# A decode-step attention and gated-FFN kernel: the tile framework's ordering replaced by the order of the source

## The chip, the cores and the metric

The kernel runs on one core of a Trainium2 chip, in one launch. The metric is device time in microseconds, lower is better. Five engines work beside one another, each through its own queue of instructions: PE (TensorE, matrix products), DVE (VectorE), ACT (ScalarE), POOL (GpSimd) and SP (SyncE, which here only issues DMA transfers). They order themselves by semaphores. Sixteen DMA engines carry the transfers between HBM and the on-chip memory SBUF; products land in PSUM.

## The reference

One token `x` of 576 numbers is normalized, and two blocks are added to it: attention of 32 heads against a cache of 8192 keys and values per head, and an FFN with 4608 units whose gate is a ReLU.

```python
def _A_ref(x, k_cache, v_cache, wq, wo):          # H, Sk, Dh = 32, 8192, 128; D = 576
    q = (x @ wq).reshape(B, Sq, H, Dh).transpose(0, 2, 1, 3)
    scores = jnp.einsum("bhqd,bhkd->bhqk", q, k_cache) * (Dh ** -0.5)
    p = _softmax(scores, axis=-1)
    o = jnp.einsum("bhqk,bhkd->bhqd", p, v_cache)
    return o.transpose(0, 2, 1, 3).reshape(B, Sq, H * Dh) @ wo

def _B_ref(x, W_gate, W_up, W_down):              # F = 4608
    gate = jnp.einsum("bsd,df->bsf", x, W_gate)
    up = jnp.einsum("bsd,df->bsf", x, W_up)
    gate = gate * (gate > 0)
    return jnp.einsum("bsf,fd->bsd", gate * up, W_down)

xn = _layernorm(x)
return x + _A_ref(xn, ...) + _B_ref(xn, ...)
```

All is float32. Each cache holds 32 x 8192 x 128 numbers, 134 MB; a unit whose gate isn't positive adds nothing, so its up and down weights needn't be read.

## The kernel before, in words

**The stream.** Nearly all bytes come through one ring of five SBUF slots (`NST = 5`, `stream`, L46 to L50). SP issues one DMA for each tile, and a slot is asked for anew when the tile in it has been used up. In the order of issue: three tiles of wq and three of the gate weights (`wg`), then for each of four groups of eight heads (`NG = 4`, `G = 8`) eight K tiles and eight V tiles of 4096 KB each, a *head tile* each, and at the end seven ever smaller tiles of wo (8, 8, 8, 4, 2, 1 and 1 heads).

**Setup and gate.** DVE normalizes x (L85 to L91) and spreads it over the partitions as `xb`. Then `dot` (L97 to L99) multiplies 128 rows of weights with it and sums: 32 dots give q (into the zero-filled `qz`), 36 give the gate for 36 chunks of 128 units (`FC = 36`). L113 to L119 make the ReLU of it (`gr`) and `idx`, the numbers of the rows to fetch; a unit with a closed gate gets a number out of range.

**FFN.** For each chunk, `fetch` (L135 to L141) has POOL gather the 128 rows of up and down weights, 4608 bytes a row, into one of three buffers `gb` (`NB = 3`); numbers out of range move nothing. `ffn(c)` (L143) then does the *up product* on DVE (`dot` with the gate as scale, result `hh`) and the *down product* on PE (`rows`, 4 products into `acc`, L129, which the profile counts as 8). `fetch` for chunk c + 3 follows it in the source.

**Attention.** `scores` (L169) multiplies a K tile by q on PE, 16 products a tile (32 in the profile, L178), for all eight heads of a group into one PSUM tile `s`. `softmax` (L183) is a chain over DVE, PE and ACT. `values` (L210) multiplies a V tile by the probabilities (L220), has DVE copy the result (`oc`, L223) and PE turn it into columns (`ot`, L225).

**What sets the order.** After every head tile the source calls `between` (L160), which puts in an `ffn` when

```python
passed += 1
if used < FC and (passed - FIRST) * FC >= (used + 1) * SPAN:
    ffn(used)
```

with `FIRST = 4` and `SPAN = 58`. The text of the source is not the order in which the engines get their instructions, though: the kernel is written in a tile framework, which records what depends on what, then arranges the instructions by a planner of its own, engine by engine, gives out the buffers and sets the semaphores. Each engine then takes its queue strictly in order.

Of the kernel before, what the change touches and what calls it, by code (L numbers as in the profile page):

```python
# [2 lines left out]

# [12 lines left out]
P = 128  # L16
D = 576
# [9 lines left out]
NST = 5  # L27
NB = 3
FIRST = 4
SPAN = 58  # L30
RQ = 11
RG = 12
# [3 lines left out]
@with_exitstack  # L36
def tile_block(ctx: ExitStack, tc: tile.TileContext, x, kt, vt, wq, wg, ud, wo, out):
    nc = tc.nc
    cp = ctx.enter_context(tc.tile_pool(name="cp", bufs=1))
    st = ctx.enter_context(tc.tile_pool(name="st", bufs=NST))  # L40
    wk = ctx.enter_context(tc.tile_pool(name="wk", bufs=2))
    pk = ctx.enter_context(tc.tile_pool(name="pk", bufs=2, space=bass.MemoryType.PSUM))
    pv = ctx.enter_context(tc.tile_pool(name="pv", bufs=1, space=bass.MemoryType.PSUM))
    ps = ctx.enter_context(tc.tile_pool(name="ps", bufs=2, space=bass.MemoryType.PSUM))

    def stream(src):  # L46
        n = src.shape[-1]
        t = st.tile([P, n], F32, tag="st", name="st")
        nc.sync.dma_start(t, src)
        return t  # L50

    xa = cp.tile([1, D], F32, name="xa")
    nc.scalar.dma_start(xa, x)
    x4 = cp.tile([P, Q], F32, name="x4")
    nc.gpsimd.memset(x4, 0.0)
    nc.scalar.dma_start(x4[0:P:32, :], x.rearrange("o (j q) -> (o j) q", j=4))
    ident = cp.tile([P, P], F32, name="ident")
    make_identity(nc, ident)

    num = cp.tile([P, FC], F32, name="num")  # L60
    nc.gpsimd.iota(num, pattern=[[P, FC]], base=0, channel_multiplier=1, allow_small_or_imprecise_dtypes=True)
    eps = cp.tile([1, 1], F32, name="eps")
    nc.vector.memset(eps, EPS)
    one = cp.tile([1, P], F32, name="one")
    nc.vector.memset(one, 1.0)
    hs = cp.tile([P, G], F32, name="hs")
    nc.vector.reduce_sum(hs, ident.rearrange("p (j i t) -> p i j t", j=4, i=G), axis=AX.XY)
    sb = cp.tile([P, 4], F32, name="sb")
    nc.vector.reduce_sum(sb, ident.rearrange("p (j m) -> p m j", j=4)[:, :4, :], axis=AX.X)
    qz = cp.tile([P, H, 63], F32, name="qz")  # L70
    nc.gpsimd.memset(qz, 0.0)
    gb = [cp.tile([P, 2 * D], F32, name=f"gb{i}") for i in range(NB)]
    for t in gb:
        nc.gpsimd.memset(t, 0.0)  # L74
    po = [pv.tile([P, 512], F32, name=f"po{i}") for i in range(2)]
    acc = pv.tile([P, 512], F32, name="acc")
    for t in po + [acc]:
        nc.vector.memset(t, 0.0)


    sm = cp.tile([1, 8], F32, name="sm")
    xb = cp.tile([P, D], F32, name="xb")
    jk = cp.tile([P, D], F32, name="jk")
    xn = jk[:1, :]
    nc.vector.reduce_sum(sm[:, 0:1], xa, axis=AX.X)  # L85
    nc.vector.tensor_scalar_mul(sm[:, 1:2], sm[:, 0:1], 1.0 / D)
    nc.vector.tensor_scalar(xa, xa, sm[:, 1:2], None, op0=ALU.subtract)  # L87
    nc.scalar.activation(xn, xa, AF.Square, accum_out=sm[:, 2:3])
    nc.scalar.activation(sm[:, 3:4], sm[:, 2:3], AF.Sqrt, bias=eps, scale=1.0 / D)
    nc.vector.reciprocal(sm[:, 4:5], sm[:, 3:4])  # L90
    nc.vector.tensor_scalar_mul(xn, xa, sm[:, 4:5])  # L91
    for b in range(2):
        px = ps.tile([P, 512], F32, tag="sm", name="px")
        nc.tensor.matmul(px[:, :D // 2], one, xn[:, b * (D // 2):(b + 1) * (D // 2)], start=True, stop=True)  # L94
        nc.vector.tensor_copy(xb[:, b * (D // 2):(b + 1) * (D // 2)], px[:, :D // 2])

    def dot(rows, dst, scale=1.0):  # L97
        nc.vector.tensor_tensor_reduce(out=jk, in0=rows, in1=xb, scale=scale, scalar=0.0,  # L98
                                       op0=ALU.mult, op1=ALU.add, accum_out=dst)  # L99

    for s in range(0, H, RQ):
        n = min(RQ, H - s)
        t = stream(wq[:, s * D:(s + n) * D])
        for i in range(n):
            dot(t[:, i * D:(i + 1) * D], qz[:, s + i, 31:32])
    gate = cp.tile([P, FC], F32, name="gate")
    for s in range(0, FC, RG):
        t = stream(wg[:, s * D:(s + RG) * D])
        for i in range(RG):
            dot(t[:, i * D:(i + 1) * D], gate[:, s + i:s + i + 1])  # L110


    gr = cp.tile([P, FC], F32, name="gr")  # L113
    nc.vector.tensor_scalar(gr, gate, 0.0, None, op0=ALU.is_gt)
    nc.vector.tensor_mul(gr, gr, gate)
    off = cp.tile([P, FC], F32, name="off")
    nc.vector.tensor_scalar(off, gate, 0.0, float(2 * F), op0=ALU.is_le, op1=ALU.mult)
    idx = cp.tile([P, FC], I32, name="idx")
    nc.vector.tensor_add(idx, off, num)  # L119
    hh = cp.tile([P, FC], F32, name="hh")  # L120
# [4 lines left out]
    def rows(t, i, col):  # L125
        nonlocal done
        for j in range(4):
            c = i + j * Q
            nc.tensor.matmul(acc[32 * j:32 * j + 1, :Q], col, t[:, c:c + Q],  # L129
                             start=(done == 0), stop=(done == total - 1))  # L130
        done += 1

    fetched = 0

    def fetch():  # L135
        nonlocal fetched
        c = fetched
        t = gb[c % NB]
        nc.gpsimd.indirect_dma_start(t, None, ud, bass.IndirectOffsetOnAxis(ap=idx[:, c:c + 1], axis=0),  # L139
                                     bounds_check=F - 1, oob_is_err=False)  # L140
        fetched += 1  # L141

    def ffn(c):  # L143
        t = gb[c % NB]
        dot(t[:, :D], hh[:, c:c + 1], gr[:, c:c + 1])
        rows(t, D, hh[:, c:c + 1])

    def turned(rows, n):
        m = n // P
        pt = ps.tile([P, 4, P], F32, tag="sm", name="pt")  # L150
        for b in range(m):
            nc.tensor.transpose(pt[:, b, :], rows[:, b * P:(b + 1) * P], ident)  # L152
        return pt

    os = cp.tile([P, H], F32, name="os")
    used = 0

    passed = 0

    def between():  # L160
        nonlocal used, passed
        passed += 1
        if used < FC and (passed - FIRST) * FC >= (used + 1) * SPAN:
            ffn(used)
            used += 1
            if fetched < FC:
                fetch()

    def scores(g):  # L169
        s = pk.tile([P, 512], F32, tag="pk", name="s")  # L170
        for i in range(G):
            h = G * g + i
            t = stream(kt[h])
            for u in range(4):
                r = 4 * i + u
                for j in range(4):
                    c = (4 * u + j) * 512
                    nc.tensor.matmul(s[32 * j:32 * j + 32, :], qz[:, h, 31 - r:63 - r], t[:, c:c + 512],  # L178
                                     start=(r == 0), stop=(r == 31))
            between()  # L180
        return s

    def softmax(g, s):  # L183
        mr = wk.tile([P, 1], F32, name="mr")
        nc.vector.reduce_max(mr, s, axis=AX.X)  # L185
        pm = ps.tile([P, 512], F32, tag="sm", name="pm")
        nc.tensor.transpose(pm[:1, :P], mr, ident)
        hm = wk.tile([1, G], F32, name="hm")
        nc.vector.tensor_reduce(hm, pm[:1, :P].rearrange("p (j i t) -> p i j t", j=4, i=G), axis=AX.XY, op=ALU.max)
        hr = wk.tile([1, 4, G, 4], F32, name="hr")  # L190
        nc.vector.tensor_scalar_mul(hr, hm[:, None, :, None].to_broadcast([1, 4, G, 4]), -SCALE)
        pb = ps.tile([P, 512], F32, tag="sm", name="pb")
        nc.tensor.matmul(pb[:, :1], hr.rearrange("p j i t -> p (j i t)"), one[:, :1], start=True, stop=True)
        nb = wk.tile([P, 1], F32, name="nb")
        nc.vector.tensor_copy(nb, pb[:, :1])  # L195
        p = wk.tile([P, 512], F32, name="p")
        lr = wk.tile([P, 1], F32, name="lr")
        nc.scalar.activation(p, s, AF.Exp, bias=nb, scale=SCALE, accum_out=lr)  # L198
        pt = turned(p, 512)
        pT = wk.tile([P, P, 4], F32, name="pT")  # L200
        nc.vector.tensor_copy(pT, pt.rearrange("k b r -> k r b"))  # L201
        lb = wk.tile([P, P], F32, name="lb")
        nc.vector.tensor_copy(lb, lr.to_broadcast([P, P]))
        pl = ps.tile([P, 512], F32, tag="sm", name="pl")
        nc.tensor.matmul(pl[:, :G], lb, hs, start=True, stop=True)
# [24 lines left out]
    for _ in range(NB):  # L230
        fetch()
# [43 lines left out]
```

## Time and profile before

| what | value |
|---|---|
| time, median of 3 runs | 777.56 us (775.14 to 777.75) |
| time of the profiled execution | 777.12 us |
| its span, first to last instruction | 775.3 us |
| mean TensorE clock granted | 0.762 of full |
| busy: PE, DVE, POOL | 407.1, 122.3, 43.0 us |
| moved by DMA | 308.83 MB, 398 GB/s on the mean |

All stretches in the profile are in microseconds from the start of the span. Busy times say little by themselves here, as transfers and engines work at once; what counts is who waits for whom at which time, and whether the DMA engines have something to do. In a line such as "PE a L178 <- DMA b", the engine on the left stood idle until the one on the right was done. A group of instructions is named by its line, its engine, what it writes, an arrow and what it reads.

### The profile page before, as it was taken

The page shows a single profiled execution, that of the slowest core. Times are in us where ns is not written, and L with a number is a line of the kernel's source. Part 1 is how long each engine was busy: PE and PEld are TensorE (multiplying, and loading weights), DVE is VectorE, ACT ScalarE, POOL GpSimd, SP SyncE. Part 2 cuts the span into 40 slices and gives each one's busy share as a digit, 9 for nine tenths or more (in the row PEclk, how much of TensorE's full clock was granted, in tenths as well). Part 3 has the DMA queues.
Part 4 walks back from the last instruction along what each step waited for, and adds up shares of the span by engine and source line. Part 5 has one row for each costly group of instructions (what it writes and reads, how often), then busy time and mean ns, then how long its engine had stood idle before and what let it go on. Part 6 is the DMA issues. An engine that isn't in the chain of part 4 may idle for free.

```text
span 775.3 us, 6515 instructions
## 1 busy us (share of the span) xinstructions
PE 407.1 (53%) x2888; PEld 118.1 (15%) x2888; DVE 122.3 (16%) x291; ACT 8.0 (1%) x14; POOL 43.0 (6%) x48
## 2 busy tenths in 40 slices
PE   1003012234357855656666765566667656667664
PEld 0000000001112311111112211112121111121123
DVE  7994011112221100000100000001000000010000
ACT  2000000000000000000000000000000000000000
POOL 2001012233310000000000000000000000000000
PEclk9997556666679986686787677777786786786789
DMA  9999977786779999999999999999999999999995
GB/s 383 433 434 430 431 315 278 291 301 253 269 274 434 430 430 428 429 431 430 430 429 432 429 430 433 430 431 432 432 433 432 433 430 433 430 429 428 430 428 216
DMA packets 16317, 308.83 MB, mean 398 GB/s; under 512 B 4150, under 2 KB 4158, under 8 KB 6818
## 3 DMA queue, kind: packets, MB, share of 16 engines
q1 hardware_dynamic: 11096, 297.93, 90.0%
q0 software_dynamic: 5184, 10.49, 4.1%
q8 instruction: 22, 0.36, 0.2%
q14 instruction: 5, 0.04, 0.0%
q10 hardware_dynamic: 10, 0.00, 0.0%
HBM read 319.16 MB, written 0.00 MB: 412 GB/s over the span
## 4 chain that ended last, share of the span: by engine, by line
DMA 72%; PE 14%; DVE 10%; issue 2%; ACT 1%; POOL 0%; POOLq 0%; DVEq 0%; ACTq 0%
DMA st<-in_kt 33%; DMA gb<-in_ud,idx 16%; DMA st<-in_vt 16%; DVE jk L98 8%; PE po L220 7%; DMA st<-in_wo 6%; PE s L178 6%; PE ot L225 1%; PE acc L129 1%; DVE oc L223 0%; DVE xa L87 0%; PE pt L152 0%; ACT p L198 0%; PE px L94 0%; POOL gb L139 0%
## 5 line engine op out<-in xcount | busy, mean ns | idle before, releaser
L178 PE MATMUL s<-st,qz 128*32 128x512 f32 x1024 | 176.8, 854 | 138.7 <-DMA st<-in_kt 138.7
L220 PE MATMUL po<-st,pT 128*4 128x512 f32 x1024 | 161.2, 786 | 57.6 <-DMA st<-in_vt 55.0
L178 PEld LDWEIGHTS s<-st,qz 128*32 128x32 f32 x1024 | 41.3, 150 | 267.3 <-DMA st<-in_kt 111.4
L129 PE MATMUL acc<-gb,hh 128*1 128x144 f32 x288 | 19.1, 353 | 115.9 <-DVE hh L98 115.9
L223 DVE COPY oc<-po 128x512 f32<-128x512 f32 x32 | 22.1, 692 | 249.0 <-PE po L220 249.0
L220 PEld LDWEIGHTS po<-st,pT 128*4 128x4 f32 x1024 | 28.4, 102 | 162.2 <-issue 102.3
L98 DVE CUSTOM_DVE_ANT_0 jk<-st,xb 128x576 f32<-128x576 f32 x68 | 51.5, 757 | 2.4
L98 DVE CUSTOM_DVE_ANT_0 jk<-gb,xb,gr 128x576 f32<-128x576 f32 x36 | 29.5, 819 | 131.1 <-DMA gb<-in_ud,idx 130.4
L225 PE MATMUL ot<-sb,oc 128*128 128x1 f32 x256 | 33.7, 253 | 26.2 <-DVE oc L223 26.2
L139 POOL DMA_INDIRECT gb<-in_ud,idx x36 | 37.3, 1037 | 179.9 <-DVE idx L119 62.3
L225 PEld LDWEIGHTS ot<-sb,oc 128*128 128x128 f32 x256 | 31.0, 191 | 56.6 <-DVE oc L223 56.6
L185 DVE TENSOR_REDUCE mr<-s 128x1 f32<-128x512 f32 x4 | 2.8, 692 | 231.5 <-PE s L178 231.5
L129 PEld LDWEIGHTS acc<-gb,hh 128*1 128x1 f32 x288 | 4.4, 81 | 132.7 <-DVE hh L98 130.3
L129 PE MATMUL acc<-st,os 128*1 128x144 f32 x256 | 10.0, 313 | 7.0 <-DMA st<-in_wo 7.0
L198 ACT ACTIVATE p<-s,nb 128x512 f32<-128x512 f32 x4 | 2.7, 687 | 665.3 <-DVE nb L195 665.3
L129 PEld LDWEIGHTS acc<-st,os 128*1 128x1 f32 x256 | 6.5, 91 | 10.2 <-DMA st<-in_wo 8.3
L94 PE MATMUL px<-jk,one 1*128 1x288 f32 x4 | 2.3, 722 | 9.8 <-DVE jk L91 9.8
L152 PE MATMUL pt<-ident,p 128*128 128x128 f32 x16 | 3.5, 360 | 4.4 <-ACT p L198 4.4
L201 DVE COPY pT<-pt 128x512 f32<-128x512 f32 x4 | 2.8, 692 | 2.9 <-PE pt L152 2.9
L87 DVE TENSOR_SCALAR xa<-xa,sm 1x576 f32<-1x576 f32 x1 | 3.1, 3056 | 0.0
L74 POOL MEMSET gb<- 128x1152 f32 x3 | 3.0, 1047 | 0.0
L98 DVE DVE_READ_ACCUMULATOR2_ANT hh<- 128x1 f32 x36 | 3.0, 83 | 0.0
(48 smaller groups left out, 35.5 us busy)
## 6 DMA issues: line engine op xcount, KB each, us to landing
st<-in_kt SPq DMA_DIRECT2D x32, 4096.0 KB, 42.4
st<-in_vt SPq DMA_DIRECT2D x32, 4096.0 KB, 42.5
st<-in_wg SPq DMA_DIRECT2D x3, 3456.0 KB, 35.4
st<-in_wo SPq DMA_DIRECT2D x3, 2304.0 KB, 35.2
st<-in_wq SPq DMA_DIRECT2D x2, 3168.0 KB, 13.9
st<-in_wq SPq DMA_DIRECT2D x1, 2880.0 KB, 23.8
st<-in_wo SPq DMA_DIRECT2D x1, 1152.0 KB, 25.3
gb<-in_ud,idx POOLq DMA_INDIRECT x36, 11.7
```

The costliest lines, as they stand in the source:

```text
L74: nc.gpsimd.memset(t, 0.0)
L87: nc.vector.tensor_scalar(xa, xa, sm[:, 1:2], None, op0=ALU.subtract)
L98: nc.vector.tensor_tensor_reduce(out=jk, in0=rows, in1=xb, scale=scale, scalar=0.0, op0=ALU.mult, op1=ALU.add, accum_out=dst)
L129: nc.tensor.matmul(acc[32 * j:32 * j + 1, :Q], col, t[:, c:c + Q], start=(done == 0), stop=(done == total - 1))
L139: nc.gpsimd.indirect_dma_start(t, None, ud, bass.IndirectOffsetOnAxis(ap=idx[:, c:c + 1], axis=0), bounds_check=F - 1, oob_is_err=False)
L152: nc.tensor.transpose(pt[:, b, :], rows[:, b * P:(b + 1) * P], ident)
L178: nc.tensor.matmul(s[32 * j:32 * j + 32, :], qz[:, h, 31 - r:63 - r], t[:, c:c + 512], start=(r == 0), stop=(r == 31))
L185: nc.vector.reduce_max(mr, s, axis=AX.X)
L201: nc.vector.tensor_copy(pT, pt.rearrange("k b r -> k r b"))
L220: nc.tensor.matmul(o[32 * j:32 * j + 4, :], pT[:, row, :], t[:, c:c + 512], start=(u == 0), stop=(u == 3))
L223: nc.vector.tensor_copy(oc, o)
L225: nc.tensor.matmul(ot[:, i:i + 1], oc[:, b * P:(b + 1) * P], sb[:, b:b + 1], start=(b == 0), stop=(b == 3))
```

## The change

The same products, sums and transfers are issued without the framework. A class `Plan` takes each instruction with the names of what it reads and writes, and keeps every engine's instructions in the order in which the source gives them. Its `finish` works out which instruction must wait for which: not for one that the engine already knows to be done through an earlier wait, and on one engine not for reads before a write, nor at all on PE; a write after a write or a read after a write on DVE, ACT or POOL is waited for. All buffers are laid out by hand; those of the softmax are now single.

`between` has a new rule (`FIRST = 6`, `EVERY = 1.55`): the up product of chunk u goes out after head tile 6 + 1.55 u or the next one, its down product one head tile later, and the gather for chunk u + 3 right behind the down product. In `values`, the turning of a tile's result (`gather(i - 1)`, a name for the L225 products and no DMA) stands behind the products of the next tile. The normalized x is kept in `xa`; `hs`, `sb` and the clearing of three PSUM tiles come after the gate. The order of the stream and its five slots are as before. At the end SP waits for the output's transfer. The core of the diff:

```diff
+    def finish(self):
+        ops = self.ops
+        known = {e: {} for e in self.eng}
+        after = []
+        place = {e: 0 for e in self.eng}
+        for n, op in enumerate(ops):
+            e = op["engine"]
+            k = known[e]
+            waits = {}
+            for o, kind in sorted(op["needs"], reverse=True):
+                of = ops[o]
+                if of["sem"] is not None:
+                    key, at = ("dma", o), 1
+                else:
+                    if of["engine"] == e and (kind == "war" or e == "PE"):
+                        continue
+                    key, at = of["engine"], of["place"]
+                if k.get(key, 0) >= at:
+                    continue
+                waits[key] = max(waits.get(key, (0, 0)), (at, o))
+                for key2, at2 in after[o].items():
+                    k[key2] = max(k.get(key2, 0), at2)
+                k[key] = max(k.get(key, 0), at)
+            op["waits"] = [o for _, o in waits.values()]
+            place[e] += 1
+            op["place"] = place[e]
+            after.append(dict(k))
...
+        for n, op in enumerate(ops):
+            engine = self.eng[op["engine"]]
+            waits = [ops[o]["value"] for o in op["waits"]]
+            for s, v in waits[1:]:
+                engine.wait_ge(s, v)
+            i = op["emit"](engine)
+            if waits:
+                i.wait_op(*waits[0], "sem-ge")
+            if "value" in op:
+                i.then_inc(op["value"][0], 16 if op["sem"] is not None else 1)
...
 NST = 5
 NB = 3
-FIRST = 4
-SPAN = 58
 RQ = 11
 RG = 12
+FIRST = 6
+EVERY = 1.55
...
     def stream(src):
+        nonlocal tiles
+        s = tiles % NST
+        tiles += 1
         n = src.shape[-1]
-        t = st.tile([P, n], F32, tag="st", name="st")
-        nc.sync.dma_start(t, src)
-        return t
+        add("SP", lambda e: e.dma_start(slot[s][:, :n], src), writes=[("st", s)], sem=slot_sem[s])
+        return slot[s], ("st", s)
...
-    def dot(rows, dst, scale=1.0):
-        nc.vector.tensor_tensor_reduce(out=jk, in0=rows, in1=xb, scale=scale, scalar=0.0,
-                                       op0=ALU.mult, op1=ALU.add, accum_out=dst)
+    def dot(rows, key, dst, dkey, scale=1.0, extra=()):
+        add("DVE", lambda e: e.tensor_tensor_reduce(out=jk, in0=rows, in1=xb, scale=scale, scalar=0.0, op0=ALU.mult,
+                                                    op1=ALU.add, accum_out=dst),
+            reads=[key, ("xb", 0), ("xb", 1), *extra], writes=[dkey, "jk"])
...
-    def fetch():
-        nonlocal fetched
-        c = fetched
-        t = gb[c % NB]
-        nc.gpsimd.indirect_dma_start(t, None, ud, bass.IndirectOffsetOnAxis(ap=idx[:, c:c + 1], axis=0),
-                                     bounds_check=F - 1, oob_is_err=False)
-        fetched += 1
-    def ffn(c):
-        t = gb[c % NB]
-        dot(t[:, :D], hh[:, c:c + 1], gr[:, c:c + 1])
-        rows(t, D, hh[:, c:c + 1])
+    def fetch(c):
+        b = c % NB
+        add("POOL", lambda e: e.indirect_dma_start(gb[b], None, ud, bass.IndirectOffsetOnAxis(ap=idx[:, c:c + 1], axis=0),
+                                                   bounds_check=F - 1, oob_is_err=False),
+            reads=["idx"], writes=[("gb", b)], sem=gb_sem[b])
+    def up(c):
+        b = c % NB
+        dot(gb[b][:, :D], ("gb", b), hh[:, c:c + 1], ("hh", c), scale=gr[:, c:c + 1], extra=["gr"])
+    def down(c):
+        b = c % NB
+        rows(gb[b], D, hh[:, c:c + 1], [("gb", b), ("hh", c)])
+        if c + NB < FC:
+            fetch(c + NB)
     passed = 0
+    ups = downs = 0
     def between():
-        nonlocal used, passed
+        nonlocal passed, ups, downs
         passed += 1
-        if used < FC and (passed - FIRST) * FC >= (used + 1) * SPAN:
-            ffn(used)
-            used += 1
-            if fetched < FC:
-                fetch()
+        if downs < ups:
+            down(downs)
+            downs += 1
+        if ups < FC and passed >= FIRST + EVERY * ups:
+            up(ups)
+            ups += 1
...
+    def values(g):
+        def gather(i):
+            o = oc[i % 2]
+            for b in range(4):
+                add("PE", lambda e, b=b: e.matmul(ot[:, i:i + 1], o[:, b * P:(b + 1) * P], sb[:, b:b + 1], start=(b == 0), stop=(b == 3)),
+                    reads=[("oc", i % 2), "sb"], writes=["ot"])
...
-            oc = wk.tile([P, 512], F32, name="oc")
-            nc.vector.tensor_copy(oc, o)
-            for b in range(4):
-                nc.tensor.matmul(ot[:, i:i + 1], oc[:, b * P:(b + 1) * P], sb[:, b:b + 1],
-                                 start=(b == 0), stop=(b == 3))
+                    add("PE", lambda e, j=j, row=row, c=c, t=t, o=o, u=u: e.matmul(o[32 * j:32 * j + 4, :], pT[:, row, :], t[:, c:c + 512],
+                                                                              start=(u == 0), stop=(u == 3)),
+                        reads=[key, "pT"], writes=[okey])
+            add("DVE", lambda e, o=o, i=i: e.tensor_copy(oc[i % 2], o), reads=[okey], writes=[("oc", i % 2)])
+            if i == 0:
+                sums(g)
+            else:
+                gather(i - 1)
             between()
-        nc.vector.tensor_mul(os[:, G * g:G * g + G], ot, rl)
-    for _ in range(NB):
-        fetch()
+        gather(G - 1)
+        add("DVE", lambda e: e.tensor_mul(os[:, G * g:G * g + G], ot[:, :G], rl), reads=["ot", "rl"], writes=[("os", g)])
...
+    out_sem = sem("out")
+    add("SP", lambda e: e.dma_start(out.rearrange("o (j q) -> (o j) q", j=4), res[0:P:32, :]), reads=["res"], writes=["out"], sem=out_sem)
+    pl.finish()
+    nc.sync.wait_ge(out_sem, 16)
```

## Prediction before the result was known

> **What bounds the kernel now.** I read the page's time lines first, because the kernel moves 308.83 MB for one output row.
>
> ```profile
> span 775.3 us, 6515 instructions
> ...
> DMA  9999977786779999999999999999999999999995
> GB/s 383 433 434 430 431 315 278 291 301 253 269 274 434 430 430 428 429 431 430 430 429 432 429 430 433 430 431 432 432 433 432 433 430 433 430 429 428 430 428 216
> ...
> q1 hardware_dynamic: 11096, 297.93, 90.0%
> q0 software_dynamic: 5184, 10.49, 4.1%
> ```
>
> The digits are the busy share of the 16 DMA engines in 40 slices of 19.4 us. They are full from the start and again from the thirteenth slice to the end; seven slices in between are not. q1 is the stream of weight, K and V tiles, q0 the gathered rows of the up and down weights. A table by stage turns this into numbers (a stretch, its length, busy time and count of instructions of PE, PEld, DVE, ACT and POOL, then the TensorE clock granted, the DMA share and GB/s):
>
> ```profile
> 0.00:5.00 5.00, 0.00 (x0) 0.00 (x0) 3.92 (x8) 1.28 (x1) 4.42 (x11) 1.00 0.70 244
> 5.00:70.00 65.00, 8.70 (x36) 2.77 (x36) 56.04 (x147) 3.63 (x5) 2.40 (x4) 0.99 1.01 432
> 70.00:110.00 40.00, 1.98 (x24) 0.32 (x24) 2.48 (x6) 0.00 (x0) 4.94 (x5) 0.50 1.00 426
> 110.00:230.00 120.00, 45.53 (x468) 12.31 (x472) 27.29 (x66) 0.00 (x0) 31.25 (x30) 0.67 0.71 265
> 230.00:740.00 510.00, 329.82 (x2036) 92.70 (x2032) 30.75 (x61) 3.11 (x8) 0.00 (x0) 0.76 1.00 431
> 740.00:760.00 20.00, 13.16 (x140) 5.08 (x132) 1.55 (x3) 0.00 (x0) 0.00 (x0) 0.87 0.99 421
> 760.00:775.30 15.30, 7.89 (x192) 4.91 (x192) 0.31 (x1) 0.00 (x0) 0.00 (x0) 0.89 0.41 163
> ```
>
> So the transfers are the bound: 431 GB/s for 510 us on end, with PE busy 330 of them. The one hole is 110 to 230 us: a share of 0.71, that is 120 x 0.29 = 34.8 us in which no DMA engine had work. Why is it there? The view of the gather buffers and the waits say:
>
> ```profile
> L98 DVE CUSTOM_DVE_ANT_0 jk<-gb,xb,gr x36: 817/819/821, 84.1 to 227.7; 128x576 f32<-128x576 f32 x36
> ```
> ```profile
> DVE jk L98 <- DMA gb<-in_ud,idx: 130.4, 25, 16.5
> PE acc L129 <- DVE hh L98: 115.9, 29, 18.4
> SPq L49 <- PE s L178: 165.6, 26, 20.5
> ```
>
> All 36 up products (L98 on gb) run between 84.1 and 227.7 us, although the loop in the source spreads them over 58 head tiles: the order in which the engines got them isn't that of the source. With three gather buffers, each group of about three waits for its gathers (130.4 us on DVE), the down products wait for DVE (115.9 us on PE), and the K products stand behind them in PE's queue. A K tile that isn't consumed keeps its slot of the ring of five, and SP can't ask for the next one (its wait on L178, up to 20.5 us, against the 9.7 us that a 4096 KB tile takes at 431 GB/s). The timeline shows one such round:
>
> ```profile
> 176.27 0.98 POOL L139 DMA_INDIRECT gb<-in_ud,idx  x1 [10.90 <-DVE hh L98]
> 177.63 5.72 PE L178 MATMUL s<-st,qz 128*32 128x512 f32 x32
> 196.64 0.82 DVE L98 CUSTOM_DVE_ANT_0 jk<-gb,xb,gr 128x576 f32<-128x576 f32 x1 [11.62 <-DMA gb<-in_ud,idx]
> 199.84 4.86 PE L178 MATMUL s<-st,qz 128*32 128x512 f32 x32
> ```
>
> Two K tiles, 22.2 us apart: the tile costs PE 5.7 us, the rest is up and down products and their gathers.
>
> **The change part by part. First, the order of the FFN work.** By the new rule, product u goes out at head tile ceil(6 + 1.55u): 6, 8, 10, 11, 13, 14, ... 61. Its down product goes out one tile later and the gather for product u + 3 right behind it. Between that gather and its use lie at least three tiles (2 down at 11, 5 up at 14), usually four: 3 x 9.7 = 29 us at the pace of the stream. How long does a gather take when the stream is full? In the chain of waits (start, length, what):
>
> ```profile
> 68.55 15.44 DMA gb<-in_ud,idx
> ...
> 85.96 26.25 DMA gb<-in_ud,idx
> ...
> 199.78 4.44 DMA gb<-in_ud,idx
> ```
> ```profile
> 94.59 0.82 DVE L98 CUSTOM_DVE_ANT_0 jk<-gb,xb,gr 128x576 f32<-128x576 f32 x1 [9.65 <-DMA gb<-in_ud,idx]
> ...
> 105.35 0.82 DVE L98 CUSTOM_DVE_ANT_0 jk<-gb,xb,gr 128x576 f32<-128x576 f32 x1 [9.93 <-DMA gb<-in_ud,idx]
> ```
>
> The first took 15.4 us, to 84.0; the products of the next two, which were asked for right behind it, could start 10.6 and 10.8 us after one another (94.59, 105.35). The one issued at 85.96 took 26.3 us, because two others were ahead of it. In a thin stretch one took 4.4. After the change one gather is asked for per 1.55 x 9.7 = 15 us, so it rarely has another ahead: 11 to 16 us, and 26 at worst, under the 29 that it has. I cost the waits at nothing. The Trainium skill, page "DMA: Bandwidth & Descriptors", section "Queues, rings and completion order", says that a DMA engine goes round its queues packet by packet, so a gather shares each engine with the stream and needn't outlast the tiles queued before it. The rows agree with 15.4 us. Served in order of asking, a gather would come after them; that is the first rival below.
>
> **PE's part of a tile.** Nothing is added to PE but its order changes: the output columns of V tile i (`gather(i - 1)`) now stand behind the products of tile i + 1, so that DVE's copy lies beside PE work.
>
> ```profile
> 85.00 0.66 PE L129 MATMUL acc<-gb,hh 128*1 128x144 f32 x8 [18.40 <-DVE hh L98]
> ```
> ```profile
> 232.47 0.70 DVE mr L185
> ...
> 236.98 5.10 PE po L220 x32
> ...
> 242.84 1.05 PE ot L225 x8
> 243.90 3.59 PE po L220 x32
> ...
> 309.54 6.38 PE s L178 x32
> ```
>
> A tile's products take 3.59 us at the full clock and up to 6.38 at the lower ones; I bound them by 2 x 3.59 = 7.2 at the half clock granted from 70 to 110 us. So, all at half clock: a V tile 7.2 + 2 x 1.05 = 9.3, a K tile 7.2, a down product 0.66 per 1.55 tiles = 0.4 (it ran at 0.50 already), a softmax of 236.98 - 232.47 = 4.5 us per 16 tiles = 0.3. The mean is 8.2 + 0.4 + 0.3 = 8.9 us for a tile, under the 9.7 of its transfer. The copy taken off the path is therefore worth nothing, and neither is a slow clock a cost, as long as the ring is full. What is late next is always the stream.
>
> **The waits that are added.** The new plan lets every dot wait for the one before (all write jk), by a semaphore. Behind a waiting dot stand the other dots, and for them waits SP, which wants their slot.
>
> ```profile
> 65.51 0.76 DVE L98 CUSTOM_DVE_ANT_0 jk<-st,xb 128x576 f32<-128x576 f32 x1
> 66.20 0.08 DVE L98 DVE_READ_ACCUMULATOR2_ANT gate<- 128x1 f32 x1
> 66.31 0.76 DVE L98 CUSTOM_DVE_ANT_0 jk<-st,xb 128x576 f32<-128x576 f32 x1
> ...
> 67.10 0.80 SPq L49 DMA_DIRECT2D st<-in_kt  x2
> ```
>
> The dots run 0.80 us apart with 0.03 between the end of one pair and the next; the gap may already hold such a wait. So the wait costs between nothing and, as a generous bound, three such gaps, 0.1 us: 0 to 7 us over 68 dots, and I take nothing, by the nearest row. Its cover: the six weight tiles are 20.05 MB, 46.5 us of stream, and four K tiles asked for before the last dot add 39, so the queue is fed until about 2 + 46.5 + 39 = 88 us, and the next request leaves at 67.1. It may come 20 us later, 0.3 us a dot, before a DMA engine idles. Cost: nothing. The same cover holds for the setup instructions moved behind the gate products (hs, sb, the memsets of PSUM), and for the gate's mask and index, which now come in another order.
>
> **Ends.** The tiles are asked for in the same order through the same five slots, and the last wo tile still waits for the rows of the second one, so I leave the tail as it is.
>
> ```profile
> 757.54 5.76 SPq L49 DMA_DIRECT2D st<-in_wo  x2
> ...
> 772.76 0.66 SPq L245 DMA_DIRECT2D out_y<-res  x1
> ```
>
> The output's transfer and the end take 775.3 - 772.76 = 2.5 us, and 777.12 - 775.3 = 1.8 lie outside the span. The framework's own closing steps are in these 4.3 us and go; what replaces them is one wait for the output. I count 0, with 1 us to either side.
>
> **The sum.** If the hole goes, every byte moves at a full queue. Bytes that aren't gathered: 308.83 - 10.49 = 298.34 MB at 431 GB/s = 692.2 us. Head: 0 to 5 us moved 5 x 0.244 = 1.22 MB, worth 2.8 us, so 2.2 are lost. Tail: 740 to 775.3 moved 20 x 0.421 + 15.3 x 0.163 = 10.9 MB, worth 25.3, so 10.0 are lost. The span is 704.4 us plus 36 gathers at a price p of DMA time. For p there are three rows. From 70 to 110 us, with the stream full, 17.04 MB moved while some 3.7 gathers of 0.291 MB landed; the other 15.96 MB are worth 37.0 us, which leaves 3.0 / 3.7 = 0.80 us. The q0 row: 4.1% of 775.3 = 31.8 us / 36 = 0.88. And 110 to 230: 85.2 busy us, 31.8 MB, of which 32.3 gathers are 9.4; 22.4 MB are worth 52.0, which leaves 33.2 / 32.3 = 1.03, in a stage where gathers often ran alone. Below none of these lies 0.291 MB / 431 = 0.68. I take 0.88, in the middle: 704.4 + 31.7 = 736.1, and with 1.8 outside **738 us** for an execution like the profiled one. That one (777.12) is 0.4 under the median of the runs shown, so I leave it there. Over the bounds of p the sum runs from 704.4 + 24.5 + 1.8 = 730.7 to 704.4 + 37.1 + 1.8 = 743.3; with the ends, 730 to 744. The step down of 39 us is the 34.8 idle ones and some 4 because a gather beside a full stream is cheaper than in the hole.
>
> **The rivals.** *The gathers are late in new places.* If gathers needed more than the 29 to 39 us between request and use, as they would behind the 42.4 us from issue to landing of a K tile, the up product would hold DVE, the down product PE, and the ring would drain at each of 36 places, though the four tiles ahead pay for most of it. For it: 26.3 us in one row; against: that one had two others ahead. If half of the idle 34.8 us came back, 738 + 17 = 755 us.
>
> ```profile
> st<-in_kt SPq DMA_DIRECT2D x32, 4096.0 KB, 42.4
> ...
> gb<-in_ud,idx POOLq DMA_INDIRECT x36, 11.7
> ```
>
> *Each gather takes more from the stream once it runs beside full queues* (the slower end). Before, four of 36 did so for certain; now all do, spread over 600 us. It makes the kernel slower by over 0.5% (781) from the p at which 704.4 + 36p + 1.8 is above that: p = 2.08 us. If a gather held the engines for the 4.4 us that it takes in a thin stretch, it would be 704.4 + 158 + 1.8 = 864 us, the far end. Against it stands the measured 0.80 in just that condition, if on four gathers only. The Trainium skill gives in "DMA: Bandwidth & Descriptors", section "Anatomy of one DMA — SWDGE (gpsimd) path", about 2.0 us fixed per transfer issued by GpSimd and its bytes at 436 GB/s, so 2.7 us a gather and 803 us for the kernel as an estimate; were that engine time, this rival would hold. The page itself calls most of it waiting for the completion, and the 0.80 agrees.
>
> *The hole isn't made by the order.* If the ring ran dry because PE is slow after each pause (the clock is 0.50 to 0.67 there), the same stretch would be as thin in source order, and the time within 0.5% of 777. Against it: with a mean clock of 0.76 the stage from 230 to 740 us moved its full 431, and a tile at half clock costs PE 8.9 us, as worked out above.
>
> **How the numbers follow.** The full stream has 0.78 (730 to 744), late gathers 0.13 (744 to 765), the order not being the cause 0.05 (775 to 780), the dear gather 0.04 (over 781). The predicted time is 738; the range 730 to 752 holds the first and part of the second. Faster by over 0.5% 0.91, within 0.5% (about what a measurement of this kernel can tell from no change) 0.05, slower by over 0.5% 0.04.
>
> **What would show it.** The DMA row full from the second slice to the last but one, and 425 to 431 GB/s between 110 and 230 us; up products one per about 15 us from some 115 to 690 us; DVE's waits for gb gone from the top (it may wait, but for nothing that is late); SP's longest wait for PE under 10 us; PE idle for in_kt and in_vt in every tile. It is wrong if the share falls under 0.95 in any 50 us between 5 and 740, or if a stretch with a share of 1.00 moves under 415 GB/s: then p is wrong. An end that is 3 us longer or shorter from the last wo tile on would show the ends mis-sized.

## The result and the profile after

The changed kernel takes 731.48 us (median of 4 runs, 729.85 to 731.79) against 777.15 for the one before (4 runs): a ratio of 0.9412, 95% interval 0.939 to 0.9435. Its profiled execution took 731.79 us with a span of 730.5. The page's time lines, which before had seven thin slices:

```profile
span 730.5 us, 6297 instructions
...
DMA  9999999999999999999999999999999999999995
GB/s 374 432 436 429 431 429 430 434 428 431 428 426 428 433 426 431 427 427 436 426 427 432 428 432 427 428 429 430 429 424 437 424 434 424 428 432 430 428 426 219
...
q1 hardware_dynamic: 11096, 297.93, 95.1%
q0 software_dynamic: 5184, 10.49, 3.7%
```

The same packets and bytes move, and no slice between the first and the last is thin. The table by stage (a stretch, its length, the busy time of five engines, the TensorE clock, the DMA share, GB/s) has the former hole in its second row, and the tail in its last:

```profile
70.00:110.00 40.00, 20.48 (x128) 4.73 (x120) 2.03 (x5) 0.00 (x0) 1.81 (x2) 0.83 1.00 428
110.00:230.00 120.00, 74.06 (x513) 21.82 (x513) 13.25 (x30) 0.78 (x2) 6.20 (x7) 0.82 1.01 430
230.00:690.00 460.00, 284.12 (x1839) 75.95 (x1843) 42.49 (x98) 2.33 (x6) 26.75 (x27) 0.76 1.00 429
690.00:730.50 40.50, 26.70 (x380) 12.43 (x368) 2.55 (x5) 0.00 (x0) 0.00 (x0) 0.86 0.79 332
```

From 110 to 230 us the share went from 0.71 to 1.01 (full; the view's shares can read a little over 1) and the rate from 265 to 430 GB/s. The stretch moved 265 x 120 = 31.8 MB before, which at 430 GB/s takes 74 us; so 46 us were lost there, and the whole gain is 45. The view of the gather buffers shows where the FFN work went, the waits what is left of it:

```profile
L198 DVE CUSTOM_DVE_ANT_0 jk<-gb,xb,gr x36: 768/810/821, 84.2 to 682.7; 128x576 f32<-128x576 f32 x36
...
DMA to landing us min/median/max: 15.1/15.7/34.4
```
```profile
DVE oc L321 <- PE po L318: 277.2, 32, 11.9
...
PE sc L279 <- DMA st<-in_kt: 183.7, 32, 48.0
...
DVE jk L198 <- DMA gb<-in_ud,idx: 170.8, 14, 19.5
...
PE po L318 <- DMA st<-in_vt: 106.5, 30, 5.1
```

The 36 up products (now L198) are spread from 84 to 683 us. PE no longer waits for DVE before a down product; it waits for a K tile 32 times and for a V tile 30 times, as an engine should beside a stream that is the bound. DVE still stands 170.8 us before gathers, and that is the point to learn from this list: a long wait isn't a cost. DVE's queue takes the next up product and sits on it, and nothing that was ready stood behind: all 32 copies of V tiles (L321) still waited for PE. In experiment 2 below the same kind of wait does cost time. Around one down product the timeline reads:

```profile
121.06 5.34 PE L279 MATMUL sc<-st,qz 128*32 128x512 f32 x32 [4.59 <-DMA st<-in_kt]
126.21 0.43 PE L232 MATMUL acc<-gb,hh 128*1 128x144 f32 x8
...
126.94 0.99 POOL L238 DMA_INDIRECT gb<-in_ud,idx  x1 [54.83 <-PE acc L232]
130.98 5.34 PE L279 MATMUL sc<-st,qz 128*32 128x512 f32 x32 [4.34 <-DMA st<-in_kt]
```

Two K tiles 9.9 us apart, not 22.2, with 4.3 us of PE's time free between them.

### The profile page after: what moved, and what is told of

It is laid out like the page before. It is cut to its first block, busy times and chain, and to the rows that moved or that the text cites. A ratio compares the mean times of both kernels' runs of the same rounds, so it can differ in the third digit from the quotient of the medians.

```text
span 730.5 us, 6297 instructions
## 1 busy us (share of the span) xinstructions
PE 413.0 (57%) x2888; PEld 117.4 (16%) x2888; DVE 120.7 (17%) x291; ACT 8.0 (1%) x14; POOL 41.7 (6%) x48
## 3 DMA queue, kind: packets, MB, share of 16 engines
q1 hardware_dynamic: 11096, 297.93, 95.1%
q0 software_dynamic: 5184, 10.49, 3.7%
## 4 chain that ended last, share of the span: by engine, by line
DMA 79%; PE 11%; DVE 8%; issue 0%; ACT 0%; DVEq 0%
DMA st<-in_vt 37%; DMA st<-in_kt 36%; DVE jk L198 7%; DMA st<-in_wo 6%; PE po L318 5%; PE sc L279 5%; DVE xa L186 0%; PE acc L232 0%; PE wa L193 0%; DMA xa<-in_x 0%; ACT L188 0%; PE wa L267 0%; PE wb L193 0%; ACT p L294 0%; ACT jk L187 0%
## 5 line engine op out<-in xcount | busy, mean ns | idle before, releaser
L279 PE MATMUL sc<-st,qz 128*32 128x512 f32 x1024 | 178.5, 861 | 183.7 <-DMA st<-in_kt 183.7
L318 PE MATMUL po<-st,pT 128*4 128x512 f32 x1024 | 172.9, 837 | 108.3 <-DMA st<-in_vt 106.5
L279 PEld LDWEIGHTS sc<-st,qz 128*32 128x32 f32 x1024 | 39.7, 151 | 310.2 <-DMA st<-in_kt 202.8
L321 DVE COPY oc<-po 128x512 f32<-128x512 f32 x32 | 22.1, 692 | 277.2 <-PE po L318 277.2
L198 DVE CUSTOM_DVE_ANT_0 jk<-gb,xb,gr 128x576 f32<-128x576 f32 x36 | 29.2, 810 | 170.8 <-DMA gb<-in_ud,idx 170.8
L198 DVE CUSTOM_DVE_ANT_0 jk<-st,xb 128x576 f32<-128x576 f32 x68 | 51.5, 758 | 3.0
L307 PEld LDWEIGHTS ot<-sb,oc 128*128 128x128 f32 x256 | 30.8, 191 | 26.2 <-issue 26.2
L286 DVE TENSOR_REDUCE mr<-sc 128x1 f32<-128x512 f32 x4 | 2.8, 692 | 122.4 <-PE sc L279 122.4
L232 PE MATMUL acc<-gb,hh 128*1 128x144 f32 x288 | 15.2, 285 | 0.0
L294 ACT ACTIVATE p<-sc,nb 128x512 f32<-128x512 f32 x4 | 2.7, 687 | 620.7 <-DVE nb L293 620.7
L267 PE MATMUL wa<-ident,p 128*128 128x128 f32 x16 | 3.1, 324 | 4.2 <-ACT p L294 4.2
L296 DVE COPY pT<-wa 128x512 f32<-128x512 f32 x4 | 2.8, 691 | 6.7 <-PE wa L267 6.7
L198 DVE DVE_READ_ACCUMULATOR2_ANT hh<- 128x1 f32 x36 | 3.0, 83 | 0.0
## 6 DMA issues: line engine op xcount, KB each, us to landing
gb<-in_ud,idx POOLq DMA_INDIRECT x36, 15.7
```

What stands on the lines that cost most here:

```text
L198: add("DVE", lambda e: e.tensor_tensor_reduce(out=jk, in0=rows, in1=xb, scale=scale, scalar=0.0, op0=ALU.mult, op1=ALU.add, accum_out=dst) ...
L232: add("PE", lambda e, j=j, c=c: e.matmul(acc[32 * j:32 * j + 1, :Q], col, t[:, c:c + Q], start=first, stop=last), reads=reads, writes=["acc"])
L267: add("PE", lambda e, b=b: e.transpose(wa[:, b * P:(b + 1) * P], p[:, b * P:(b + 1) * P], ident), reads=["p", "ident"], writes=["wa"])
L279: add("PE", lambda e, h=h, r=r, j=j, c=c, t=t: e.matmul(s[32 * j:32 * j + 32, :], qz[:, h, 31 - r:63 - r], t[:, c:c + 512], start=(r == 0) ...
L286: add("DVE", lambda e: e.reduce_max(mr, s, axis=AX.X), reads=[skey], writes=["mr"])
L296: add("DVE", lambda e: e.tensor_copy(pT, wa.rearrange("k (b r) -> k r b", b=4)), reads=["wa"], writes=["pT"])
```

## The experiments

Two theories at first. **A**: the order of the FFN work in the queues made the hole, and nothing else in the change counts. **B**: the framework's own waits and steps cost the time. Later ones ask what a gather costs and where the tail's time goes. Ratios are to the kernel before, run beside each on the same chip.

**1. The new kernel with the old order.** What the engines had before is put back into the hand-ordered kernel: bunches behind the first seven K tiles.

```diff
+BUNCH = (4, 5, 6, 6, 6, 6, 3)
...
-        if downs < ups:
-            down(downs)
-            downs += 1
-        if ups < FC and passed >= FIRST + EVERY * ups:
-            up(ups)
-            ups += 1
+        for _ in range(BUNCH[passed - 1] if passed <= len(BUNCH) else 0):
+            up(ups)
+            down(ups)
+            ups += 1
```

> The kernel after, with only the placing of the FFN pairs put back to what the engines had before: 4, 5, 6, 6, 6, 6 and 3 pairs of up and down products behind the first seven K tiles. Theory A (the order alone made the hole): the hole between 110 and 230 us comes back, DMA share about 0.7 there, time 770 to 780 us. Theory B (the framework's own waits and closing steps cost the time): it stays at 730 to 735 us.

776.47 us, ratio 0.9997 (0.9979 to 1.0014). The hole is back in the same place and depth:

```profile
110.00:230.00 120.00, 44.97 (x448) 12.17 (x448) 26.60 (x65) 0.00 (x0) 32.38 (x30) 0.66 0.69 257
```
```profile
DVE jk L199 <- DMA gb<-in_ud,idx: 130.1, 25, 13.6
PE acc L233 <- DVE hh L199: 117.6, 24, 18.8
```

A holds: the whole gain is the order, since everything else of the change is still in this kernel and gains nothing by itself.

**2. The framework with the down products pinned.** In the kernel before, a line tells the planner to queue each pair's PE work behind the head tile that precedes it in the source.

```diff
-            ffn(used)
+            with tc.issue_after(last.ins):
+                ffn(used)
```

`last` is the last matmul of the head tile.

> The kernel before, still in the framework, with each down product pinned behind the head tile that stands ahead of it in the source. Theory A: the hole goes with the bunch, 730 to 740 us, unless DVE's queue still has up products ahead of copies they hold up. Theory B: 770 to 778 us.

748.7 us, ratio 0.9626 (0.9582 to 0.9671): neither figure, 28 us of the 45. The reservation in the expectation was the case. The planner still chose DVE's order, and put up products ahead of copies of V tiles. The timeline at one such place:

```profile
221.66 1.04 PE L221 MATMUL po<-st,pT 128*4 128x512 f32 x8
...
234.80 0.82 DVE L98 CUSTOM_DVE_ANT_0 jk<-gb,xb,gr 128x576 f32<-128x576 f32 x1 [17.00 <-DMA gb<-in_ud,idx]
...
235.54 0.69 DVE L224 COPY oc<-po 128x512 f32<-128x512 f32 x1
236.28 1.87 PE L226 MATMUL ot<-sb,oc 128*128 128x1 f32 x8 [13.59 <-DVE oc L224]
```

DVE sat 17 us before a gather while the copy behind it had been ready since 222.7, and PE waited 13.6 us for that copy. Over the run PE stood 179.5 us before such copies, part of it covered by the ring; the second fence has the 26.2 of the kernel before:

```profile
PE ot L226 <- DVE oc L224: 179.5, 32, 14.7
```
```profile
PE ot L225 <- DVE oc L223: 26.2, 32, 0.8
```

What was left of the wait had moved from PE's queue to DVE's, and the page's time line still has thin slices, now spread over the run:

```profile
DMA  9999999999998999999999699999999699999996
```

**3. The framework with both pinned.** The up product too, behind the copy before it.

```diff
-            with tc.issue_after(last.ins):
+            with tc.issue_after(last.ins), tc.issue_after(lastd.ins):
                 ffn(used)
```

`lastd` is that copy (in the K stages, the last DVE instruction of the stage before).

> The kernel before, in the framework, with the down product pinned on PE (as in the run that pinned it alone and took 749 us) and the up product pinned on DVE behind the copy of the V tile that stands ahead of it. Theory A, in the form that every queue's order counts: the rest of the holes goes as well, 730 to 736 us. Theory B (what was left was the framework's own cost): 745 to 752 us.

733.32 us, ratio 0.9445 (0.9432 to 0.9457). The changed kernel, run beside it, took 731.49 (0.9419, 0.9406 to 0.9433). The framework with two constraints on its order is within 1.8 us of the kernel without it:

```profile
5.00:230.00 225.00, 114.19 (x673) 31.82 (x677) 71.00 (x181) 4.41 (x7) 11.48 (x12) 0.80 1.00 430
230.00:690.00 460.00, 306.81 (x1859) 81.26 (x1855) 42.16 (x96) 2.33 (x6) 26.10 (x26) 0.70 1.01 429
690.00:732.30 42.30, 28.68 (x365) 12.41 (x356) 3.28 (x7) 0.00 (x0) 0.00 (x0) 0.74 0.76 317
```

Up to 690 us its rates are those of the changed kernel. The rest is behind that: 42.3 us against 40.1 in the one beside it (its row stands in experiment 9), and outside the span 1.9 (734.2 - 732.3) against 1.3. What makes its tail 2 us longer was not tried.

**4. The lag of one tile.** The down product directly behind its up product, in the hand-ordered kernel.

```diff
-        if downs < ups:
-            down(downs)
-            downs += 1
         if ups < FC and passed >= FIRST + EVERY * ups:
             up(ups)
+            down(ups)
             ups += 1
```

> The kernel after, with the down product directly behind its up product instead of a head tile later. PE then waits about 1 us for DVE at 36 places, while a tile has at least 0.8 us to spare. Theory A: no change, 730 to 733 us. If the lag of a tile is part of the gain: over 735 us.

731.65 us, ratio 0.9417 (0.939 to 0.9444): no change. The lag is worth nothing here; the stream covers PE's waits for the up product (19 of them, 12.3 us in all, 1.3 at the longest).

**5. One pair for every tile.**

```diff
-EVERY = 1.55
+EVERY = 1.0
```

> The kernel after with an FFN pair at every head tile from the sixth on, 36 in a row, in place of one per 1.55 tiles: a gather per 9.7 us, with a lead of 19.5 us. If gathers under a full stream come one after another at 10.7 us each, as three did before, each falls 1 us further behind, and the stream thins until they keep up: 733 to 760 us. If a gather only takes 15.7 us and several go at once: 730 to 733 us.

732.01 us, ratio 0.9419 (0.9381 to 0.9456): no change either. The gathers just keep up; they overlap, and each takes longer:

```profile
L238 POOL DMA_INDIRECT gb<-in_ud,idx x36: 989/992/1456, 66.6 to 466.2; - x36
...
DMA to landing us min/median/max: 15.4/18.1/34.3
```

So the exact spacing doesn't matter: bunches of three to six a tile hurt, one a tile doesn't. What lies between wasn't run.

**6. No lead for the gathers.** `NB = 3` to `NB = 1`: a gather is asked for only when the product before it is done.

> The kernel after with one gather buffer in place of three, so that no gather has a lead: it is asked for when the product before it is done, and takes 15.7 us at the median. One pair per 17.5 us (15.7 + 0.85 + about 1) against one per 15.1 (1.55 tiles). The first rival of the prediction (late gathers) at its strongest: up to 36 x 2.4 = 86 us more, less as the stream thins and gathers come faster: 745 to 790 us. If the five tiles of the ring pay for the lateness: 730 to 735 us.

757.31 us, ratio 0.9731 (0.9691 to 0.9771). This is the first rival of the prediction, made to happen. Late in the run the timeline shows its period, and the view of the gather buffer the time to landing:

```profile
642.10 0.82 DVE L198 CUSTOM_DVE_ANT_0 jk<-gb,xb,gr 128x576 f32<-128x576 f32 x1 [16.98 <-DMA gb<-in_ud,idx]
642.98 0.66 PE L232 MATMUL acc<-gb,hh 128*1 128x144 f32 x8 [7.73 <-DVE hh L198]
...
643.94 0.99 POOL L238 DMA_INDIRECT gb<-in_ud,idx  x1 [16.82 <-PE acc L232]
660.23 0.82 DVE L198 CUSTOM_DVE_ANT_0 jk<-gb,xb,gr 128x576 f32<-128x576 f32 x1 [17.30 <-DMA gb<-in_ud,idx]
```
```profile
DMA to landing us min/median/max: 4.1/15.5/17.4
```

One pair per 18 us, while the plan wants one per 15. The loss is 26 us, not 36 x 2.4 = 86. Over the whole run a pair took 17.5 us here (the first down product at 126.2, the last at 737.2) against 16.2 in the changed kernel (126.2 to 693.5), so the last is 44 us late, not 86; five of the 36 gathers found a thin stream and landed in 4.1 to 9.3 us. That the ring's tiles cover the rest, 44 to 26, is argued.

**7. The price of a gather.** The first three gathers only; the other 33 chunks use the rows that are there.

```diff
-        if c + NB < FC:
+        if c + NB < NB:
```

> The kernel after with the first three gathers only; the other 33 chunks use the rows already there. The price of a gather beside a full stream is what goes, by 33: at 0.68 us (its bytes alone) 709 us, at 0.80 (the stretch from 70 to 110 us of the kernel before) 705, at 0.88 (taken in the prediction) 702.5, at the 2.7 of the page 642.

704.6 us, ratio 0.9065 (0.903 to 0.91). 731.48 - 704.60 = 26.9 us for 33 gathers, **0.81 us each**. That is next to the 0.80 read from the stretch of 70 to 110 us of the kernel before, and under the 0.88 that the prediction took. The agreement with 0.80 is partly luck: the end is 3 us shorter here (experiment 9), so beside the running stream the price is nearer 24 / 33 = 0.72, little over the 0.68 of the bytes alone. The packet records of the changed kernel say the same: 2275 rows at a median of 0.178 us and 2909 packets of 4 bytes at 0.009 make about 27 us of all 16 engines, 0.75 a gather. From the Trainium skill, page "DMA: Bandwidth & Descriptors", section "Anatomy of one DMA — SWDGE (gpsimd) path", the prediction had worked out an estimate of 2.7 us a gather; as time taken from the stream the runs refute it. Whether its fixed 2 us are part of the time to landing no run here shows.

**8. Every gather twice**, the second into one scratch buffer.

```diff
             reads=["idx"], writes=[("gb", b)], sem=gb_sem[b])
+        add("POOL", lambda e: e.indirect_dma_start(gx, None, ud, ...),
+            reads=["idx"], writes=["gx"], sem=gx_sem)
```

> The kernel after with every gather made a second time, into a buffer that nothing reads. 36 more gathers: at 0.68 us each 756 us, at 0.80 760, at 0.88 763; more, if a gather is late because its double stands ahead of it (two take about 26 us under a full stream, and the lead is 29).

783.39 us, ratio 1.0084 (1.005 to 1.0118): 52 us more, not 25 to 32. As a measure of the price it failed, because the single scratch buffer made POOL wait for each double before it could ask for the next gather:

```profile
POOL gx L243 <- DMA gx<-in_ud,idx: 522.1, 34, 23.0
```
```profile
327.06 0.99 POOL L243 DMA_INDIRECT gx<-in_ud,idx  x1 [19.30 <-DMA gx<-in_ud,idx]
...
348.02 0.99 POOL L243 DMA_INDIRECT gx<-in_ud,idx  x1 [18.67 <-DMA gx<-in_ud,idx]
```

What it does show is the pace: beside a full stream two gathers take 21.0 us, 10.5 each, and this kernel's rule wants two per 15.1 us. So the gathers fell behind, and the stream ran dry in the second half of the run, as the page's rate shows:

```profile
GB/s 388 431 433 426 429 427 428 430 427 428 429 428 426 430 429 427 425 436 423 430 428 420 428 360 383 373 428 433 370 432 345 430 360 412 419 426 172 409 428 299
```

Of the 52 us, 36 x 0.81 = 29 are the price and the other 23 the lateness; this split is worked out, not measured.

**9. Equal shares of the gathered rows, and the shape of the tail.** The tail of the changed kernel loses 9.3 us against the full rate; that of experiment 7, with 3 gathers, only 6.3 (13.2 us at 224 GB/s are worth 6.9 us at 431):

```profile
690.00:703.20 13.20, 7.63 (x184) 5.18 (x174) 0.31 (x1) 0.00 (x0) 0.00 (x0) 0.87 0.55 224
```

A gather takes the rows whose gates are open, and these may load the DMA engines unequally. This kernel fetches every second row instead, and so leaves out rows that the output needs.

```diff
-    add("DVE", lambda e: e.tensor_scalar(off, gate, 0.0, float(2 * F), op0=ALU.is_le, op1=ALU.mult), reads=gates, writes=["off"])
+    add("DVE", lambda e: e.reduce_sum(par, ident.rearrange("p (m t) -> p t m", t=2), axis=AX.X), reads=["ident"], writes=["par"])
+    add("DVE", lambda e: e.tensor_scalar_mul(off.rearrange("p (m t) -> p m t", t=2), par[:, None, :].to_broadcast([P, FC // 2, 2]), float(2 * F)),
+        reads=["par", *gates], writes=["off"])
```

> The kernel after with rows fetched by a fixed pattern, every second one, 64 of 128 in each gather, in place of those whose gate is open (which the output needs). Nearly the same bytes (2304 rows against about 2276). Theory C: the DMA engines get unequal shares of the gathered rows, and the last one ends some 3 us behind the mean; with equal shares these 3 us go from the tail: 728 to 729 us. Theory D (the tail is longer for another reason): 731.5 to 732.5 us.

A second kernel asks whether the late request of the last wo tile holds the end: `for n in (8, 8, 8, 6, 2)`.

> The kernel after with the wo tiles of 8, 8, 8, 6 and 2 heads, so that none has to wait for the rows of another wo tile. If the late request of the last tile holds the end: 1 to 3 us less, 728.5 to 730.5. If the stream's last bytes hold it: the same or 1 us more for the two heads at the end, 731 to 733 us.

And the changed kernel beside both:

> The kernel after, unchanged, as the measure for the two kernels above on the same chip: 730 to 732 us.

The unchanged kernel took 731.49 us (0.9419, 0.9406 to 0.9433). Equal rows: 729.33 (0.9395, 0.9383 to 0.9408), 2.2 us less, where theory C said 2.5 to 3.5. Five wo tiles: 732.54 (0.9433, 0.9419 to 0.9447), no gain, if anything the 1 us more for the two heads at the end: the late request isn't what holds it. The last stage of the unchanged kernel and of the one with equal rows:

```profile
690.00:730.10 40.10, 25.21 (x376) 11.95 (x364) 2.55 (x5) 0.00 (x0) 0.00 (x0) 0.91 0.79 334
```
```profile
690.00:728.50 38.50, 25.43 (x352) 11.95 (x344) 1.86 (x4) 0.00 (x0) 0.00 (x0) 0.78 0.83 352
```

13.39 MB against 13.55: the tail loses 40.1 - 31.1 = 9.0 us in the one and 38.5 - 31.4 = 7.1 in the other, so the 2 us are gone from just there. This is what unequal loads of the DMA engines would do. The packet records don't name the engine, but they have a sign of it: the last sixteen 32 KB packets of the last V tile end over 4.8 us in the unchanged kernel, over 2.5 with equal rows and over 3.0 with three gathers. So the engines are further apart with the rows as they fall; which engine got which rows isn't shown.

## Why the prediction was right, point by point

The forecast was 738 us, in 730 to 752; measured were 731.48, near the low end.

*What bounds.* Right. The share is 1.00 to 1.01 from 5 to 690 us, and the hole of 110 to 230 us was the whole gain. Experiment 1 brings it back by order alone, experiment 3 takes it away by order alone, within 1.8 us.

*The gathers have enough lead.* Right: 15.7 us at the median (11 to 16 forecast, 29 to be had). The 34.4 us at most is the third of the first three, which are asked for together; in experiment 7, where there are no others, they took 15.6, 24.9 and 34.4:

```profile
DMA to landing us min/median/max: 15.6/24.9/34.4
```

PE's first down product is at 126 us, long after them. Experiment 6 shows what the first rival is worth where the lead is taken away: 26 us. The prediction's 17 was of that order by luck: it took half of the idle 34.8 us without a reason for the half.

*PE's part.* Right: a tile leaves PE idle for the stream. The columns of a tile behind the next tile's products, and the down product a tile later, were costed at nothing; experiment 4 confirms the second, and no run tried the first alone.

*The added waits on DVE.* Right. Before, SP could ask for the fifth and sixth K tile at 67.10; now:

```profile
66.89 0.76 DVE L198 CUSTOM_DVE_ANT_0 jk<-st,xb 128x576 f32<-128x576 f32 x1
...
67.68 0.80 SPq L165 DMA_DIRECT2D st<-in_kt  x2
```

0.6 us later over 68 dots, of 20 that were free.

*The sum.* Its total is 6.2 us too high against the profiled execution (738.0 against 731.79), and the mis-sized term is **the price of a gather**, where the text said "I take 0.88, in the middle". With the stage table of the kernel after, the tail loses 9.3 (10.0 counted), 1.3 lie outside the span (1.8 counted), and 730.5 - 692.2 - 2.2 - 9.3 = 26.8 us are left for 36 gathers, 0.74 each in place of 31.7 us in all. So 4.9 of the 6.2 us are the price, 0.7 the tail, 0.5 the end. Experiment 7 gives 0.81 with the gathers' share in the tail, and the queue's own row after says 3.7% of 730.5 = 27.0 us, 0.75. Of the prediction's three rows only the first (0.80) was taken beside a full stream, which is the condition after the change; the other two (0.88, 1.03) hold the thin stretch, where the same packets had a larger share (4.1% of 775.3 us before, 3.7% of 730.5 after). The row with the right condition should have been taken, not the middle one: 704.4 + 36 x 0.80 + 1.8 = 735.0. Even that is 3.2 us too high, as it rested on 3.7 gathers. The same term explains why the step down was 45.3 us and not 39: the 34.8 idle us went as forecast, but the gathers became cheaper by some 10 us, not 4.

*The dear gather* is refuted by 0.81 us, and with it the estimate of 2.7 us as engine time. *The order not being the cause* is refuted by experiment 1.

*The signs.* The full DMA row and 430 GB/s came as said, and PE's waits in 62 of the 64 tiles. Three didn't. The up products begin at 84 us, not 115, since nothing but the gather holds the first of them. DVE's wait for the gathers isn't gone from the top: it grew from 130.4 to 170.8 us, though for nothing that was late. And SP's longest wait for PE is 12.3 us, not under 10; the gathers aren't the cause, as the kernel of experiment 7 has 12.8, and what is stays open. None cost time.

## What to carry to other kernels

Where a planner orders the queues, look in the trace at when a group of instructions really runs, against where the source puts it: here 36 pairs meant for 58 tiles ran behind the first seven. In-order queues make a side task with a slow input dangerous on every engine that it touches, so it must be spread, with its input asked for early, on all of them: pinning it on PE alone gave 28 of 45 us, and the wait reappeared on DVE. And before a rewrite without the framework, try to pin the order in it: two constraints got to within 1.8 us of the hand-ordered kernel.

## What the runs showed of the hardware

A gather of some 0.29 MB costs a full stream 0.72 to 0.81 us (experiment 7) but needs 15.7 us to land beside it, and 4.1 at the least when the stream is thin (experiment 6). Beside a full stream two gathers took 21.0 us (experiment 8), so about 10.5 us a gather is the pace; one per head tile (experiment 5) was still carried. The packet counts suggest why: a gather has 5184 / 36 = 144 packets, nine for each of 16 engines, and a tile of the stream has 11096 / 77 = 144 as well (6 weight tiles, 64 head tiles and 7 of wo). The 32 KB packets of a head tile take 1.22 us each. If an engine takes a packet of each queue in turn, a gather lasts about as long as the tile beside it, by an estimate 8 x 1.22 + 0.75 = 10.5 us, whatever its bytes; the packets of the gather issued at 126.94 us start from 131.0 to 142.2. No run changed the packets, so this isn't shown. And which rows were fetched, at nearly the same bytes, changed the end by 2.2 us (experiment 9).
